# Queries and keys of pairs 4 to 9 loaded by casting DMAs, the third weight issued earlier, and the feed-forward units around the second batch dealt differently

## The chip, the cores and the metric

The kernel runs on one core of one Trainium2 chip. The metric is the device time of one execution in microseconds (us). Engines are named as in the profile: PE (TensorE), DVE (VectorE), ACT (ScalarE), POOL (GpSimd), SP (SyncE). SP and ACT issue hardware DMAs, POOL issues software DMAs, and only POOL's convert the type on the way.

## The reference

Attention with a few extra keys ("beacons") in front, causal over the rest, is followed by a feed-forward layer that takes the largest of three products.

```python
B, H, S, Nb, D = (8, 8, 576, 16, 64)
k_all = np.concatenate([beacon_k, k], axis=2)
v_all = np.concatenate([beacon_v, v], axis=2)
scores = (1.0 / np.sqrt(D)) * np.matmul(q, k_all.transpose(0, 1, 3, 2))
scores = np.where(causal, -1000000000.0, scores)      # beacons always visible
a = np.exp(scores - scores.max(-1, keepdims=True))
a /= a.sum(-1, keepdims=True) + 1e-09
x = np.matmul(a, v_all).transpose(0, 2, 1, 3).reshape(4608, 512)
h = np.maximum(np.maximum(x @ w1, x @ w2), x @ w3)    # 512 -> 768
out = h @ w_out                                       # 768 -> 512
```

All inputs and the output are float32; the kernel computes in bf16 with float32 accumulation.

## The kernel before

The eight heads of a batch are taken as four *pairs* of heads, numbered through all batches: pairs 0 to 3 are batch 0, 4 to 7 batch 1, 8 to 11 batch 2 and so on to 31 (`PPB` is 4, the pairs of a batch). For each pair the kernel needs queries and keys with the head dimension on the partitions. They reach that form in one of two ways. For batches 0 to 3 PE transposes them: `turn_pair` does 12 transposes of 96 tokens each into two PSUM banks, and `evac_k` and `evac_q` copy the banks into the tiles `kT` and `qT`. From batch 4 on (`B_PE`) a DMA transposes them by way of DRAM.

From batch 1 on, a pair goes through these steps.

- `load_pair` (SP) loads q and k of the pair as float32 into a stage tile `st`, in two DMAs of 288 KB.
- `cast_pair`, or `cast_piece` once for q and once for k, converts them to bf16 on POOL (line 260) into the tiles `p160` and `p161`.
- `turn_pair` transposes (line 387), DVE and ACT copy out (lines 433 and 422).
- `emit_burst` does all 12 score matmuls of the pair (line 495) into all eight PSUM banks, in four groups of two banks; ACT takes the exponentials (line 513).
- `emit_masks` zeroes the causal triangles on POOL (line 535).
- For two pairs together ("a quad") `emit_pv_whole` does 72 matmuls with the values and with ones (line 615); ACT and DVE divide.

Values come by `load_v` on SP, in two pieces per batch, and are converted by `cast_v` on POOL (line 305). The weights come by casting DMAs from POOL: `load_w` (line 327, two DMAs per weight) and `load_w_out` (line 330, one DMA of 768 KB).

The feed-forward work is cut into a fixed list of units; `F(n)` emits the next n of them. Tokens go in blocks of 512. The list of block 0 is: units 0 to 2 (first weight, first half of the tokens, `mm1_halves`, line 720, eight matmuls of 256 columns each), 3 to 5 (second weight, first half), 6 to 11 (the same for the second half), 12 to 17 (third weight, `mm1_unit`, line 691, four matmuls of 512 columns and a maximum on DVE at line 709), 18 to 21 (`mm2_unit`, line 739, six matmuls of 512 columns with `w_out`). Every later block has 22 units too, and their order on PE is the order of emission.

The whole order is written by hand: `start`, `first_batch` (batch 0 in finer steps), `second_batch` (batch 1), then a loop over pairs 8 to 31 that fills the space between the bursts with units up to a fixed count per pair. Each engine takes its own instructions strictly in the order of emission, so a POOL instruction that waits holds up every POOL instruction behind it, DMA issues among them. Eight semaphores serve POOL's DMAs in turn: the issue of a DMA waits until the one eight before it has landed.

In the trace of before, the parts around the change come in this order on PE: the last two products of batch 0 with values, units 3 and 4, the transposes of pair 4, unit 5, and then for each of pairs 4 to 7 a burst, the next pair's transposes and two units (after pair 7's burst: four units, then `emit_pv_whole` for pairs 4 and 5, the transposes of pair 8, two units). Pair 8's burst, `emit_pv_whole` for pairs 6 and 7, unit 18 (the first with `w_out`), the transposes of pair 9 and unit 19 follow.

Of the kernel before, what the change touches and what calls it, by code (L numbers as in the profile page):

```python
# [17 lines left out]
def kernel(  # L18
# [85 lines left out]
    def place(p):  # L104
        b, pi = divmod(p, PPB)
        return b, pi // PPQ, 2 * (pi % PPQ)

    const = ctx.enter_context(tc.tile_pool(name="const", bufs=1))
    st_pool = ctx.enter_context(tc.tile_pool(name="st", bufs=8))
    pair_pool = ctx.enter_context(tc.tile_pool(name="pair", bufs=4))  # L110
    half_pool = ctx.enter_context(tc.tile_pool(name="half", bufs=2))
    v_pool = ctx.enter_context(tc.tile_pool(name="v", bufs=2))
# [105 lines left out]
    def load_pair(p, gate=None):  # L218
        b, g, j0 = place(p)
        hs = slice(head(g, j0), head(g, j0) + 2)  # L220
        st = new_stage(("pair", p))
        if gate:
            gate.memset(st[0:QP, 0:1], 0.0)
        for i, src in enumerate((q, k)):
            nc.sync.dma_start(
                out=st[0:QP, i * NQ2 : (i + 1) * NQ2].rearrange("p (h x) -> p h x", h=2),
                in_=src[b, hs].rearrange("h (p r) d -> p h (r d)", r=QR),
            )
# [14 lines left out]
    def cast_half(p, i, cast):  # L243
        t16 = half_pool.tile([QP, HR, 2, D], BF16, name=f"h16{i}")
        cast(t16.rearrange("p r h d -> p h r d"), stage.pop(("half", p, i)))
        stage["half16", p, 0, i] = (t16.rearrange("p r h d -> p r (h d)"),)

    def load_quad(g, h):
        for i in range(2):
            t16 = const.tile([QP, 4, HR, D], BF16, name=f"quad{g}{h}{i}")  # L250
            nc.gpsimd.dma_start(
                out=t16.rearrange("p h r d -> p h (r d)"), in_=half_source(g, h, i, 0, 4)
            )
            for j in range(PPQ):
                stage["half16", PPQ * g + j, h, i] = (t16[:, 2 * j], t16[:, 2 * j + 1])

    def cast_piece(p, i, cast):
        st = stage["pair", p]
        t16 = pair_pool.tile([QP, QR, 2, D], BF16, name=f"p16{i}")
        cast(  # L260
            t16.rearrange("p r h d -> p h r d"),
            st[0:QP, i * NQ2 : (i + 1) * NQ2].rearrange("p (h r d) -> p h r d", h=2, r=QR),
        )
        stage["pair16", p, i] = t16

    def cast_pair(p, q_cast, k_cast):
        cast_piece(p, 0, q_cast)
        cast_piece(p, 1, k_cast)
        stage.pop(("pair", p))
# [98 lines left out]
    def store_pair(p):  # L368
        b, pi = divmod(p, PPB)
        for i, dst in enumerate((q_dram[b][pi], k_dram[b][pi, Nb:NK])):  # L370
            src = stage.pop(("pair16", p, i))
            nc.sync.dma_start(
                out=dst.rearrange("(p r) x -> p (r x)", r=QR),
                in_=src.rearrange("p r h d -> p (r h d)"),
            )

    def fetch_pair(p):
# [4 lines left out]


    def turn(p, i, ps):
        src = stage.pop(("pair16", p, i))
        for r in range(QR):
            nc.tensor.transpose(  # L387
                ps[:, r * QP : (r + 1) * QP],
                src[:, r].rearrange("p h d -> p (h d)"),
                ident[0:QP, 0:QP],  # L390
            )

    def fill(at_bank, n):
        for _ in range(n):
# [274 lines left out]
    def finish_pv():  # L669
        invert_sums()  # L670
        multiply()
# [143 lines left out]
    def cast_step(p):  # L815
        return (p - 2, 0) if p < B_PE * PPB else (p - 5, int(p < 19))
# [6 lines left out]
            load_beacons(B_PE, B, bk32)  # L823
        load_pair(p, **gate)

    loads = [(cast_step(p), 2 * (p >= B_PE * PPB), partial(load_turned_pair, p)) for p in range(2 * PPB, NPAIR)]
    loads += [(v_step(b, i), 1, partial(load_v, b, i)) for b in range(2, B) for i in range(2)]
    loads = [load for _, _, load in sorted(loads, key=lambda x: x[:2])]

    def next_load(n=1, **gate):  # L830
        for _ in range(n):
            if loads:
                loads.pop(0)(**gate)
# [51 lines left out]
    def first_batch():  # L885
        S_(0, 0)
        T(2, 0, 0, 6)
        S_(1, 0)
        T(2, 0, 1, 7, None, 3)
        T(3, 0, 0, 4)  # L890
        T(3, 0, 1, 5)
        V(0)
        V(1)
        load_w(0, [0])
        fill(6, 2)
        S_(2, 0)
# [24 lines left out]
        P(0, 0, 0, 1)  # L921
        S_(1, 2)
        M(0, 3, True)
        P(0, 0, 1)
        M(1, 1)
        invert_sums()
        S_(1, 3)
        P(1, 0, apart=True)
        M(1, 2)
        invert_sums()  # L930
        multiply(3)
        M(1, 3, True)
        load_w(1, [1])
        S_(2, 1)
        by_pool(bk16_1, bk32_1)
        multiply()
        load_pair(PPB, nc.vector)
        for p in range(PPB + 1, 2 * PPB):
            load_pair(p)
        load_v(1, 0)  # L940
        load_v(1, 1)
        next_load()
        S_(2, 2)
        P(0, 1)
        S_(2, 3)
        M(2, 1)
        invert_sums()
        F()
        S_(3, 1)
        M(2, 2)  # L950
        multiply()
        F()
        S_(3, 2)
        M(2, 3, True)
        S_(3, 3)
        M(3, 1)
        M(3, 2)
        M(3, 3, True)
        F()
        turn_beacons(1, B_PE, bk16_1)  # L960
        cast_pair(PPB, by_pool, by_pool)
        P(1, 1)
        finish_pv()
        F(2)
        turn_pair(PPB, by_act)
        place_beacons(PPB, by_act)
        cast_pair(PPB + 1, by_pool, by_pool)
        load_w(2)
        F()
        free_banks[:] = [2, 3, 0, 1, 4, 5, 6, 7]  # L970

    def second_batch():
        for p in range(PPB, 2 * PPB):
            place_beacons(p + 1, by_act)
            emit_burst(p)
            for gi in range(NG):
                emit_masks(p, gi)
                if p < PPB + 2 and 0 < gi < 3:
                    cast_piece(p + 2, gi - 1, by_pool)
                if p == 2 * PPB - 1 and gi == 1:  # L980
                    cast_v(1, 1, by_pool)
                    next_load(gate=nc.gpsimd)
                    next_load(3)
            if p < PPB + 2:
                stage.pop(("pair", p + 2))
            if p == PPB + 2:
                load_w_out()
                cast_v(1, 0, by_pool)
            if p + 1 < 2 * PPB:
                turn_pair(p + 1, by_dve)  # L990
                F(2, next_psum)
        F(4, next_psum)
        for p in range(2 * PPB, 2 * PPB + 2):
            cast_pair(p, by_pool, by_pool)
            next_load()
        finish = emit_pv_whole(n_quad)
        turn_pair(2 * PPB, by_dve)
        F(2, next_psum)
        finish()
# [93 lines left out]
```

## Time and profile before

| | |
|---|---|
| median of 3 runs (lowest, highest) | 286.55 us (285.75, 287.72) |
| the profiled execution: time, span | 285.18 us, 283.5 us |
| PE busy | 274.7 us (97%), 2996 matmuls |
| DVE, ACT, POOL busy | 172.7 us, 159.4 us, 136.4 us |
| L260, the casts of q and k on POOL | 56 instructions, 44.7 us, 821 ns each |
| L387, the transposes of q and k on PE | 144 matmuls, 8.6 us |
| software DMA queue (POOL) | 4048 packets, 4.03 MB, 9.0% of 16 engines' span |
| hardware DMA queue (SP) | 80672 packets, 45.76 MB, 71.8% |

The span is the time between the first and the last profiled instruction of the program; the 1.7 us around it belong to the execution's time. PE's busy time is a model of overlapped matmuls, so a busy PE need not be at its peak; where a wait matters, the start of the next matmul says more. Stretches in the text are in us from the start of the span.

### The profile page before, as it was taken

Reading aid. Unit: us, or ns where it says so; the run is one execution under the profiler, and the core shown is the slowest. Engines: PE = TensorE matmul, PEld = TensorE weight load, DVE = VectorE, ACT = ScalarE, POOL = GpSimd, SP = SyncE. Lnnn points to the kernel's source line nnn. Section 1 sums busy time; section 2 is a strip of 40 time slices with the busy share of each in tenths; the row PEclk is TensorE's granted clock in tenths of the full one; section 3 lists DMA queues with packets and bytes.
Section 4 is the critical chain, followed back from the end, with each engine's and each line's share of the span. In section 5 each row is a group of like instructions: output and inputs, shape, how many; then the busy total and the mean of one; then the engine's idle time right before and its main releaser. Section 6 shows DMA issues by size and latency. Waiting matters only on the chain.

```text
span 283.5 us, 7622 instructions
## 1 busy us (share of the span) xinstructions
PE 274.7 (97%) x2996; PEld 156.4 (55%) x2996; DVE 172.7 (61%) x303; ACT 159.4 (56%) x299; POOL 136.4 (48%) x282
## 2 busy tenths in 40 slices
PE   7889999999999999999999999999999999999995
PEld 3466664555555555555556787555555554444442
DVE  3774765583856658274836383638363847876873
ACT  3697595896668576858585858585767640000000
POOL 7263789287376865466556746583346210000000
PEclk9999999999999999999999999999999999999999
DMA  7999999999999999999999999999451003004004
GB/s 146 193 198 222 246 225 178 240 201 295 276 226 235 255 265 203 226 222 240 250 213 225 267 254 183 216 258 218 121 156 39 0 2 146 2 1 150 0 0 148
DMA packets 85315, 50.59 MB, mean 178 GB/s; under 512 B 64416, under 2 KB 80032, under 8 KB 85280
## 3 DMA queue, kind: packets, MB, share of 16 engines
q1 hardware_dynamic: 80672, 45.76, 71.8%
q0 software_dynamic: 4048, 4.03, 9.0%
q8 instruction: 23, 0.38, 0.6%
q10 hardware_dynamic: 560, 0.33, 0.5%
q14 instruction: 12, 0.10, 0.1%
HBM read 35.13 MB, written 14.22 MB: 174 GB/s over the span
## 4 chain that ended last, share of the span: by engine, by line
PE 82%; DVE 1%; issue 0%
PE acc L691 46%; PE acc L739 16%; PE acc L615 11%; PE acc L495 7%; PE acc L387 2%; PE acc L757 0%; DVE hT L709 0%; DVE qT L422 0%; DVE y L764 0%; DVE kT L433 0%
## 5 line engine op out<-in xcount | busy, mean ns | idle before, releaser
L691 PE MATMUL acc<-xT,w_sb 128*128 128x512 bf16 (+4 forms) x744 | 135.3, 338 | 0.0
L709 DVE TENSOR_TENSOR hT<-hT,acc 128x512 bf16<-128x512 bf16 x102 | 70.0, 687 | 59.2 <-PE acc L691 50.0
L691 PEld LDWEIGHTS <-w_sb 128*128 128x128 bf16 x744 | 69.2, 98 | 59.7
L535 POOL TENSOR_SCALAR_AFFINE_SELECT at_sb<-at_sb 128x256 bf16<-128x256 bf16 (+2 forms) x176 | 62.8, 378 | 71.1 <-ACT at_sb L513 69.4
L513 ACT ACTIVATE at_sb<-acc 128x208 bf16<-128x208 f32 (+3 forms) x140 | 89.5, 737 | 5.9 <-PE acc L495 4.6
L260 POOL CAST p<-st 96x768 bf16<-96x768 f32 x56 | 44.7, 821 | 9.3 <-PE acc L615 5.1
L739 PE MATMUL acc<-w_out_sb,hT 128*128 128x512 bf16 (+2 forms) x246 | 48.4, 348 | 0.0
L711 ACT CAST hT<-acc 128x352 bf16<-128x352 f32 x18 | 8.1, 452 | 47.0 <-PE acc L691 47.0
L739 PEld LDWEIGHTS <-hT 128*128 128x128 bf16 x246 | 22.6, 98 | 21.7 <-DVE hT L709 1.6
L746 DVE COPY y<-acc 128x512 f32<-128x512 f32 (+1 forms) x35 | 21.9, 628 | 20.5 <-PE acc L739 14.8
L711 DVE CAST hT<-acc 128x512 bf16<-128x512 f32 (+1 forms) x48 | 26.6, 554 | 9.4 <-PE acc L691 9.1
L495 PE MATMUL acc<-qT,kT 64*128 64x208 bf16 (+1 forms) x336 | 26.9, 280 | 1.1 <-DVE hT L730 0.6
L764 ACT COPY y<-acc 128x320 f32<-128x320 f32 x1 | 0.4, 426 | 46.0 <-PE acc L757 46.0
L495 PEld LDWEIGHTS <-kT 64*128 64x128 bf16 x336 | 15.5, 94 | 13.3 <-issue 2.6
L615 PE MATMUL acc<-at_sb,v_sb 128*32 128x512 bf16 (+5 forms) x672 | 22.8, 281 | 0.0
L638 DVE TENSOR_TENSOR xT<-raw,recip 128x576 bf16<-128x576 f32 x28 | 21.8, 821 | 0.0
L625 ACT COPY raw<-acc 128x512 f32<-128x512 f32 x28 | 15.8, 637 | 4.5 <-PE acc L615 4.3
L305 POOL CAST v_sb<-st 128x1536 bf16<-128x1536 f32 (+2 forms) x21 | 18.3, 893 | 0.0
L615 PEld LDWEIGHTS <-v_sb 128*32 128x32 bf16 (+1 forms) x672 | 14.5, 96 | 6.7
L489 ACT ACTIVATE at_sb<-acc 128x1024 bf16<-128x1024 f32 (+3 forms) x16 | 13.1, 860 | 3.6 <-PE acc L480 3.5
L615 PE MATMUL acc<-at_sb,ones 128*32 128x512 bf16 (+3 forms) x336 | 14.9, 284 | 0.0
L433 DVE COPY kT<-acc 128x576 bf16<-128x576 bf16 x12 | 9.0, 752 | 6.3 <-PE acc L387 6.3
(69 smaller groups left out, 170.5 us busy)
## 6 DMA issues: line engine op xcount, KB each, us to landing
out_dram<-y SPq DMA_DIRECT2D x35, 256.0 KB, 3.5
st<-in_q_dram SPq DMA_DIRECT2D x28, 288.0 KB, 5.3
st<-in_k_dram SPq DMA_DIRECT2D x28, 288.0 KB, 5.5
st<-in_v_dram SPq DMA_DIRECT2D x24, 256.0 KB, 6.7
w_sb<-in_moe_w_dram POOLq DMA_DIRECT2D x6, 384.0 KB, 7.7
q_dram<-p SPq DMA_DIRECT2D x16, 144.0 KB, 2.3
k_dram<-p SPq DMA_DIRECT2D x16, 144.0 KB, 2.3
st<-in_v_dram SPq DMA_DIRECT2D x8, 224.0 KB, 6.4
```

The source lines that it names most:

```text
L260: cast(t16.rearrange("p r h d -> p h r d"), st[0:QP, i * NQ2 : (i + 1) * NQ2].rearrange("p (h r d) -> p h r d", h=2, r=QR),)
L305: cast(v_sb[0:n, t:t1].rearrange("p t h d -> p (t h d)"), st[0:n, (t - t_lo) * H * D : (t1 - t_lo) * H * D],)
L495: nc.tensor.matmul(ps, kTs[p % NT][hs, 128 * t : 128 * t + 128], qTs[p % NT][hs, q0:q1], start=True, stop=True, tile_position=(64 * e, 0),)
L513: nc.scalar.activation(out=both_heads(p, gi)[:, e0:e1], in_=acc[:, first + e0 : first + e1, 0 : g_width(p, gi)], func=AF.Exp, scale=scale,)
L535: nc.gpsimd.affine_select(out=view, in_=view, compare_op=ALU.is_ge, fill=0.0, base=x0, pattern=[[0, 2], [1, hi - lo]], channel_multiplier=-1,)
L615: nc.tensor.matmul(acc[32 * j : 32 * j + 32, bank, lo + q0 - qa : lo + qb - qa], lhsT, at_view(PPQ * quad + j // 2, t, j % 2, q0, qb), sta ...
L638: nc.vector.tensor_mul(xT[:, 2 * g + i, c0 : c0 + S], raw[:, i], recip)
L691: nc.tensor.matmul(ps[:, a:b], w_in[i][:, ct, 128 * ft : 128 * (ft + 1)], xT[:, ct, x0 : x0 + b - a], start=(ct == 0), stop=(ct == n_ct - 1),)
L709: nc.vector.tensor_max(h[:, lo:hi], h[:, lo:hi], ps[:, lo:hi])
L711: (by_act if hi < TOKB else by_dve)(h[:, lo:hi], ps[:, lo:hi])
L739: nc.tensor.matmul(ps[:, lo:hi], hT[:, ft, 128 * tt : 128 * (tt + 1)], w_out_sb[:, ft, lo:hi], start=(ft == 0), stop=(ft == n_ft - 1),)
L746: (by_act if hi < d_model else by_dve)(y[:, lo:hi], ps[:, lo:hi])
```

## The change

- `load_cast` is new. It loads q and k of a pair by two casting DMAs from POOL, 288 KB of float32 each, straight into bf16 tiles. There is no stage tile and no cast on POOL. The tiles are those that `load_quad` fills for batch 0, now two larger ones per quad that are used again by later pairs.
- Pairs 4 to 9 go this way. The loads of pairs 4 to 7 are issued in `first_batch` between POOL's masks of batch 0; those of pairs 8 and 9 at the end of `second_batch`: pair 8's right after pair 7's burst, pair 9's after `load_w_out`.
- In the new tiles each head lies by itself, so `turn` does 24 transposes of 64 columns of weights for such a pair, two side by side on the array, in place of 12 of 128.
- `load_w(2)`, the third weight, moves from behind the casts of pairs 4 and 5 to behind the load of pair 7.
- `load_w_out` moves from the end of pair 6 (before `cast_v(1, 0)`) to the middle of pair 7's masks, behind `cast_v(1, 1)`.
- `load_v` of batch 1 moves from the middle of `first_batch` to behind pair 4's transposes, gated by a DVE memset. The list of later loads starts at pair 10 rather than 8.
- Units: one unit (not two) ahead of pair 4's transposes and two (not one) behind; three instead of two after the bursts of pairs 4 and 5; two instead of four after that of pair 7. By the product of pairs 4 and 5 with the values, 16 units are out in both kernels.
- The stage pool has seven tiles instead of eight.

```diff
-    st_pool = ctx.enter_context(tc.tile_pool(name="st", bufs=8))
+    st_pool = ctx.enter_context(tc.tile_pool(name="st", bufs=7))
...
+    quads = [
+        [const.tile([QP, 2 * 4, HR, D], BF16, name=f"quad{g}{i}") for i in range(2)] for g in range(n_quad)
+    ]
+
+    def load_cast(p):
+        b, g, j0 = place(p)
+        for i, src in enumerate((q, k)):
+            t16 = quads[g][i][:, 2 * j0 : 2 * j0 + 4]
+            nc.gpsimd.dma_start(
+                out=t16.rearrange("p (h s) r d -> p h (s r d)", h=2),
+                in_=src[b, head(g, j0) : head(g, j0) + 2].rearrange("h (p r) d -> p h (r d)", r=QR),
+            )
+            rows = t16.rearrange("p (h s) r d -> p h (s r) d", h=2)
+            stage["pair16", p, i] = (rows[:, 0], rows[:, 1])
...
     def turn(p, i, ps):
-        src = stage.pop(("pair16", p, i))
+        heads = stage.pop(("pair16", p, i))
+        n = 128 // len(heads)
         for r in range(QR):
-            nc.tensor.transpose(
-                ps[:, r * QP : (r + 1) * QP],
-                src[:, r].rearrange("p h d -> p (h d)"),
-                ident[0:QP, 0:QP],
-            )
+            for e, src in enumerate(heads):
+                nc.tensor.transpose(
+                    ps[n * e : n * e + n, r * QP : (r + 1) * QP],
+                    src[:, r],
+                    ident[0:QP, 0:QP],
+                    tile_position=(0, n * e),
+                )
...
-    loads = [... for p in range(2 * PPB, NPAIR)]
+    loads = [... for p in range(2 * PPB + 2, NPAIR)]
...
         load_w(1, [1])
+        load_cast(PPB)
         S_(2, 1)
         by_pool(bk16_1, bk32_1)
         multiply()
-        load_pair(PPB, nc.vector)
-        for p in range(PPB + 1, 2 * PPB):
-            load_pair(p)
-        load_v(1, 0)
-        load_v(1, 1)
-        next_load()
         S_(2, 2)
         P(0, 1)
         S_(2, 3)
         M(2, 1)
+        load_cast(PPB + 1)
         invert_sums()
         F()
         S_(3, 1)
         M(2, 2)
+        load_cast(PPB + 2)
...
         M(3, 1)
         M(3, 2)
+        load_cast(PPB + 3)
+        load_w(2)
         M(3, 3, True)
         F()
         turn_beacons(1, B_PE, bk16_1)
-        cast_pair(PPB, by_pool, by_pool)
         P(1, 1)
         finish_pv()
+        F()
+        turn_pair(PPB, by_act)
+        load_v(1, 0, nc.vector)
+        load_v(1, 1)
+        place_beacons(PPB, by_act)
         F(2)
-        turn_pair(PPB, by_act)
-        place_beacons(PPB, by_act)
-        cast_pair(PPB + 1, by_pool, by_pool)
-        load_w(2)
-        F()
...
         for p in range(PPB, 2 * PPB):
+            last = p == 2 * PPB - 1
             place_beacons(p + 1, by_act)
             emit_burst(p)
+            if last:
+                load_cast(2 * PPB)
             for gi in range(NG):
                 emit_masks(p, gi)
-                if p < PPB + 2 and 0 < gi < 3:
-                    cast_piece(p + 2, gi - 1, by_pool)
-                if p == 2 * PPB - 1 and gi == 1:
+                if last and gi == 1:
                     cast_v(1, 1, by_pool)
+                    load_w_out()
+                    load_cast(2 * PPB + 1)
                     next_load(gate=nc.gpsimd)
-                    next_load(3)
-            if p < PPB + 2:
-                stage.pop(("pair", p + 2))
-            if p == PPB + 2:
-                load_w_out()
+                    next_load(4)
+            if p == 2 * PPB - 2:
                 cast_v(1, 0, by_pool)
-            if p + 1 < 2 * PPB:
+            if not last:
                 turn_pair(p + 1, by_dve)
-                F(2, next_psum)
-        F(4, next_psum)
-        for p in range(2 * PPB, 2 * PPB + 2):
-            cast_pair(p, by_pool, by_pool)
-            next_load()
+            F(3 if p < PPB + 2 else 2, next_psum)
         finish = emit_pv_whole(n_quad)
         turn_pair(2 * PPB, by_dve)
         F(2, next_psum)
```

More of the change, by code (lines that the diff above doesn't have):

```diff
@@ L246, in cast_half @@
         stage["half16", p, 0, i] = (t16.rearrange("p r h d -> p r (h d)"),)
+    quads = [
[11 more added lines that the diff above has]
+            stage["pair16", p, i] = (rows[:, 0], rows[:, 1])
     def load_quad(g, h):
         for i in range(2):
-            t16 = const.tile([QP, 4, HR, D], BF16, name=f"quad{g}{h}{i}")
+            t16 = quads[g][i][:, 4 * h : 4 * h + 4]
             nc.gpsimd.dma_start(
@@ L263, in cast_piece @@
         )
-        stage["pair16", p, i] = t16
+        stage["pair16", p, i] = (t16.rearrange("p r h d -> p r (h d)"),)
     def cast_pair(p, q_cast, k_cast):
@@ L370, in store_pair @@
         for i, dst in enumerate((q_dram[b][pi], k_dram[b][pi, Nb:NK])):
-            src = stage.pop(("pair16", p, i))
+            (src,) = stage.pop(("pair16", p, i))
             nc.sync.dma_start(
                 out=dst.rearrange("(p r) x -> p (r x)", r=QR),
-                in_=src.rearrange("p r h d -> p (r h d)"),
+                in_=src.rearrange("p r x -> p (r x)"),
             )
@@ L384, in turn @@
     def turn(p, i, ps):
-        src = stage.pop(("pair16", p, i))
+        heads = stage.pop(("pair16", p, i))
+        n = 128 // len(heads)
         for r in range(QR):
-            nc.tensor.transpose(
-                ps[:, r * QP : (r + 1) * QP],
-                src[:, r].rearrange("p h d -> p (h d)"),
-                ident[0:QP, 0:QP],
-            )
+            for e, src in enumerate(heads):
[5 more added lines that the diff above has]
+                )
     def fill(at_bank, n):
@@ L824, in load_turned_pair @@
         load_pair(p, **gate)
-    loads = [(cast_step(p), 2 * (p >= B_PE * PPB), partial(load_turned_pair, p)) for p in range(2 * PPB, NPAIR)]
+    loads = [(cast_step(p), 2 * (p >= B_PE * PPB), partial(load_turned_pair, p)) for p in range(2 * PPB + 2, NPAIR)]
     loads += [(v_step(b, i), 1, partial(load_v, b, i)) for b in range(2, B) for i in range(2)]
```

## The prediction

> **What bounds the kernel now.** I read the page's totals and its chain first, then PE's timeline, then POOL's beside it, then the DMA rows.
>
> ```profile
> PE 274.7 (97%) x2996; PEld 156.4 (55%) x2996; DVE 172.7 (61%) x303; ACT 159.4 (56%) x299; POOL 136.4 (48%) x282
> ...
> PE 82%; DVE 1%; issue 0%
> ```
>
> PE is busy for 97%, and the chain runs through PE from 43.7 us to the end with only a few waits between. So PE's stream is the time: a gap that is closed before the end is a gain, and every new gap is a loss that nothing later makes good. POOL, busy for 48%, is no bound in itself.
>
> ```profile
> 29.18 0.42 PE L387 MATMUL acc<-ident,p 96*128 96x96 bf16 x6
> 30.06 0.43 PE L387 MATMUL acc<-ident,p 96*128 96x96 bf16 x6 [0.47 <-POOL p L260]
> 30.33 1.04 PE L720 MATMUL acc<-xT,w_sb 128*128 128x256 bf16 x8
> ...
> 32.44 0.98 PE L387 MATMUL acc<-ident,p 96*128 96x96 bf16 x12
> 33.26 1.91 PE L720 MATMUL acc<-xT,w_sb 128*128 128x256 bf16 x16
> 35.10 0.81 PE L495 MATMUL acc<-qT,kT 64*128 64x208 bf16 x7
> 36.20 0.36 PE L495 MATMUL acc<-qT,kT 64*128 64x336 bf16 x5 [0.28 <-DVE hT L728]
> 36.50 0.69 PE L387 MATMUL acc<-ident,p 96*128 96x96 bf16 x12
> ...
> 47.57 0.87 PE L615 MATMUL acc<-at_sb,ones 128*32 128x512 bf16 x20
> ...
> 49.82 0.83 PE L387 MATMUL acc<-ident,p 96*128 96x96 bf16 x12
> ```
>
> Starts are compared. Twelve transposes take 0.52 us when nothing holds them (36.50 to 37.02). Pair 4's take 1.15 us (29.18 to 30.33) and pair 5's 0.82 (32.44 to 33.26), for POOL's casts come late. A burst takes 0.85 us later in the chain, but 1.40 in batch 1 (35.10 to 36.50), since its last bank waits for DVE's copies of the two units ahead. That is what can be won: 0.63 + 0.30, and 0.55 for each of three bursts.
>
> ```profile
> 42.48 0.93 POOL L535 TENSOR_SCALAR_AFFINE_SELECT at_sb<-at_sb 128x256 bf16<-128x256 bf16 x3 [0.60 <-ACT at_sb L513]
> 43.36 0.85 POOL L330 DMA_DIRECT2D w_out_sb<-in_moe_w_out_dram  x1
> 44.21 1.48 POOL L305 CAST v_sb<-st 128x1536 bf16<-128x1536 f32 x1
> 45.63 0.76 POOL L535 TENSOR_SCALAR_AFFINE_SELECT at_sb<-at_sb 128x256 bf16<-128x256 bf16 x2
> 46.34 1.16 POOL L305 CAST v_sb<-st 128x512 bf16<-128x512 f32 x2
> ```
>
> This is POOL around pair 7's burst (42.62 on PE). Pair 6's last masks follow ACT's last exponential at once, so POOL cannot come sooner to what stands behind them. The weight `w_out` is issued at 43.36.
>
> ```profile
> w_sb<-in_moe_w_dram POOLq DMA_DIRECT2D x6, 384.0 KB, 7.7
> ...
> w_out_sb<-in_moe_w_out_dram POOLq DMA_DIRECT2D x1, 768.0 KB, 11.4
> quad<-in_q_dram POOLq DMA_DIRECT2D x3, 144.0 KB, 7.3
> quad<-in_k_dram POOLq DMA_DIRECT2D x3, 144.0 KB, 8.1
> ```
>
> The last column is the time from issue to landing. `w_out` landed at 54.8, 1.1 us before PE's first matmul with it at 55.91. A casting DMA on POOL's queue is no quick thing.
>
> **The change part by part.** *POOL's casts of pairs 4 to 9* go: 12 of 0.82 us, 9.8 us in all. Twelve DMA issues come at 0.55 to 0.67 us (w_sb and quad rows), some 7 us. Off the path both; what counts is when data is there.
>
> *Pair 4.* Its loads are issued behind the last half of the second weight (POOL 20.1) and no stage loads compete until 30. By the slowest cast row (9.7 us) they land at 30.5, by the quad medians at 28.5; PE comes at about 28.8, so no wait is taken. That saves 0.63. Against it, four issues of pairs 5 and 6 stand before POOL's last masks of batch 0, which ended at 25.5 and move to 26.5; PE's product with values needs them at 26.2: 0.4 lost. The transposes are 24 in place of 12. The old half-width rows took 0.38 us for 12 and 0.51 for 18, so about 0.71 for 24: 0.2 more. (Bounds: 0, if two side by side cost one, and 0.25.) Pair 4's burst stays at 31.3.
>
> *To the product of pairs 4 and 5.* Pairs 5 to 7 are issued at 23.4 to 27.6 and needed at 32, 37 and 41: in time even at 9.7 us. The third weight is issued at 27.6 instead of 32.9, the last unit of the second weight needs no wait in either. With three units DVE has 2.76 us for copies instead of 1.84, and the wait in the bursts of pairs 5 and 6 falls from 0.55 to some 0.15; pair 7's, with two units ahead, keeps it. Sum: 0.30 (pair 5) and 0.8 (two bursts) won, three sets of transposes at 0.2 lost, four units moved but none added: 0.7 with the odd tenths of the unit rows (0.92 and 0.87). So the product starts at 46.9 instead of 47.64. Bounds: -2.5 if every wait goes, 0 if DVE's lag stays.
>
> *Pair 8's load* is the first loss. Pair 6's burst now starts at 40.3; ACT's exponentials end 3.55 us later (0.36 + 3.19, as in before), masks 1.0, `cast_v` 1.48: POOL comes to the two issues at 46.3 and 46.9. PE wants the data at 46.9 + 2.25 (L615) = 49.2, less than 3 us later. No cast landed in under 5.7 us, with much else in flight; the system is quiet here, and the same 288 KB on SP's queue landed in 3.4 and 3.6 us when it was (issues at 87.9 and 88.4). I take 4.1, nearer the quiet rows: k lands at 51.0 and the transposes end at 51.35, against 49.7 without a wait: 1.65 lost. Bounds: 0.95 at 3.4 us, 3.3 at 5.7.
>
> *w_out* is the second. It goes behind pair 8's two issues, two masks (0.76) and `cast_v(1, 1)` (1.16): issue at 49.4 instead of 43.4. PE comes to unit 18 at 51.35 + 5.5 (50.41 to 55.91 in before) = 56.85. The nearest rows are `w_out` itself, 11.4, and the two halves of the third weight, together the same 768 KB, 9.9 (issue at 32.88, second landing at 42.74). Middle 10.6: landing at 60.0, 3.15 lost. Bounds: nothing at 5.7 (the fastest w_sb, half the size), 4 at 11.4. The cover before was the 12.5 us from issue to use; now it is 7.4.
>
> *Pair 9's load* stands behind `w_out` in POOL's queue (50.3 to 51.4). In 5.7 us that queue moved `w_out`:
>
> ```profile
> q0 software_dynamic: 759, 0.77, 92.5%
> ```
>
> (stretch 45.8 to 51.5: packets, MB, share). So 0.29 MB more is 2.2 us: it lands near 62, and PE comes to its transposes at 61.3. With 0.2 for the transposes 0.5 is lost (0.2 to 2). SP's later loads start 2.7 us later (51 instead of 48.4) under a PE that is 4 to 5 later: nothing. The masks of pair 7 end at 52 on POOL and are needed at 54: hidden. Seven stage tiles suffice, as two pairs fewer are staged.
>
> Sum: -0.7 + 1.65 + 3.15 + 0.5 = +4.6 us. On the profiled execution that is 285.18 + 4.6 = 289.8; that execution lies 1.37 us under the median of the runs, so the median after is 286.55 + 4.6 = 291.1.
>
> Two rules of the Trainium skill beside this. "DMA: Bandwidth & Descriptors" (section on the anatomy of one DMA, SWDGE path) puts a DMA from GpSimd at about 2.0 us plus its bytes over 436 GB/s; the 1.57 MB read for `w_out` would then be 5.6 us, where the trace shows 11.4. By the rule unit 18 would not wait at all and the sum would be near +1. "TensorE: Matmul & The Clock Gate" (Part 1, the HAM clock gate) says that after an idle window of about 3.4 us the array runs at half rate until it has been busy as long; no run here shows it yet, for the granted clock is 1.00 in every stretch and no wait of PE passes 1.5 us. By that rule a wait of 3.2 us might cost up to 1.7 us more, an estimate from its figures, and the sum would be +6.3.
>
> **The rivals.** *Loads land quickly* (not slower). Pair 8's in 3.4 us, `w_out` in under 7.4, since nothing is in flight when it is issued, and only SP's loads from 51 on stretch it. For it: the bulk of `w_out`, 0.77 of 0.79 MB, went in 5.7 us, and the first 2.4 us after its issue showed one packet, with a pair's load still moving. Against it: the last packets trailed for 3.3 us under SP's loads, which now come 1.6 us after the issue rather than 4.2. Then -0.7 + 0.95 + 0.2 = +0.45: 287.0. It decides below 7.4 us from issue to landing of `w_out`.
>
> *All of PE's old gaps go and no new one comes* (faster). All of what can be won, 0.93 + 1.65, and side by side transposes free, loads in time: -2.6, or 284.0. For it: DVE's and ACT's busy shares leave room. Against it: pair 8's load comes to POOL under 3 us before its use.
>
> *POOL is held longer* (much slower). The values of batch 1 are issued at 31 instead of 28.1 and their first piece landed 15.6 us after the first issue. Again 15.6 us puts it at 46.6, POOL's cast of it waits 1.8 us, and with it pair 8, `w_out` at 11.4 and pair 9: +7.2, or 293.8. Against it: what kept those loads so long, four pairs on the same queue, is gone.
>
> **How the numbers follow.** Forecast 0.48 (own range 288.8 to 293), quick landing 0.28, longer hold 0.14, no gaps 0.10. One per cent, 2.9 us, is about what a measurement of this kernel can tell from no change; the bounds are 283.7 and 289.4. Slower: 0.14 and 0.44 of the forecast's 0.48: 0.58. Same: 0.28 and the other 0.04: 0.32. Faster: 0.10. The range runs from 286.2, under the quick landing, to 294.8, over the longer hold, and leaves out most of the no-gap case and the ends of the others. Predicted: 291.1.
>
> **What would show it.** Right: PE's line 739 starts first near 60, with a wait for the DMA of `w_out`; the transposes of pair 8 wait 1 to 2 us for a quad DMA; the product of pairs 4 and 5 starts near 46.9; bursts of pairs 5 and 6 take about 1.0 us; 24 transposes take 0.7. Wrong: `w_out` lands within 7 us of its issue, or POOL issues pair 8's load much before 46, or the bursts keep their 1.4 us, or PE's clock leaves 1.00.

## The result and the profile after

| | before | after |
|---|---|---|
| median of 6 runs (lowest, highest) | 285.98 us (285.19, 287.72) | 289.65 us (288.42, 291.65) |
| ratio of after to before, 95% interval | | 1.0127 (1.0094 to 1.0159) |
| the profiled execution: time, span | 285.18 us, 283.5 us | 290.40 us, 288.7 us |

The changed kernel is slower, by 3.7 us at the median. The prediction had named 291.1 us in a range of 286.2 to 294.8. The lines of the file have moved: the transposes of line 387 are now line 404, the score matmuls (495) line 513, the products with values (615) line 633, the units with `w_out` (739) line 757, the masks (535) line 553, the casts of values (305) line 320. The tiles of the cast queries and keys are now called `quad`.

First the totals of the page after, and the chain that ended last.

```profile
PE 277.3 (96%) x3068; PEld 157.3 (54%) x3068; DVE 172.3 (60%) x303; ACT 159.6 (55%) x299; POOL 136.7 (47%) x282
...
PE 85%; DMA 6%; POOL 2%; DVE 2%; issue 2%; ACT 1%; POOLq 0%; DVEq 0%; ACTq 0%
```

The span grew by 5.2 us and PE's busy time by 2.6, with 72 more matmuls (half-width transposes). Part of the time is therefore idle PE, and part is work that took longer. Before, the chain from 43.7 us on was PE, but for 2.7 us (50.7 to 53.4) that went through DVE's copies; now 6% of it is DMA. The chain in order of time says where: one piece is a load in the start phase, and the other this.

```profile
48.22 1.10 POOL v_sb L320 x2
50.74 9.92 DMA quad<-in_k_dram
61.15 2.65 PE acc L757 x12
```

The chain comes through a cast of values on POOL, then through the issue of pair 9's keys at 50.74 and their 9.92 us to landing. PE's timeline shows the waits themselves (start, length, line, count, and in brackets the idle time with what ended it).

```profile
28.62 0.70 PE L404 MATMUL acc<-ident,quad 96*64 96x96 bf16 x24
...
36.57 0.39 PE L513 MATMUL acc<-qT,kT 64*128 64x336 bf16 x6 [0.24 <-DVE hT L746]
...
47.07 0.86 PE L633 MATMUL acc<-at_sb,ones 128*32 128x512 bf16 x20
...
48.83 0.27 PE L633 MATMUL acc<-at_sb,v_sb 128*32 128x208 bf16 x4 [0.34 <-POOL v_sb L320]
49.38 0.90 PE L633 MATMUL acc<-at_sb,v_sb 80*32 80x80 bf16 x24 [0.28 <-POOL v_sb L320]
...
50.30 0.70 PE L404 MATMUL acc<-ident,quad 96*64 96x96 bf16 x24
...
57.22 1.47 PE L757 MATMUL acc<-w_out_sb,hT 128*128 128x512 bf16 x6 [0.82 <-DMA w_out_sb<-in_moe_w_out_dram]
59.07 0.45 PE L404 MATMUL acc<-ident,quad 96*64 96x96 bf16 x12 [0.38 <-DMA quad<-in_q_dram]
60.71 0.45 PE L404 MATMUL acc<-ident,quad 96*64 96x96 bf16 x12 [1.19 <-DMA quad<-in_k_dram]
61.08 2.72 PE L757 MATMUL acc<-w_out_sb,hT 128*128 128x352 bf16 x12
63.74 1.27 PE L513 MATMUL acc<-qT,kT 64*128 64x208 bf16 x12
```

Up to 47.07 PE has gained 0.50 us on before (47.57). Part of this comparison is the start phase, which differs from execution to execution: the first product of batch 0 with values begins at 16.40 before and 17.00 after, ahead of the first load that moved (19.68). Counted from unit 3 (27.36 and 27.65), the way to the product takes 20.21 us before and 19.42 after, so the gain of this stretch is 0.8 us. Then PE waits for POOL in the middle of the product with values, for `w_out`, and twice for pair 9. And POOL's timeline shows why each of these comes late:

```profile
44.73 1.46 POOL L320 CAST v_sb<-st 128x1536 bf16<-128x1536 f32 x1
46.14 0.67 POOL L256 DMA_DIRECT2D quad<-in_q_dram  x1
46.80 0.65 POOL L256 DMA_DIRECT2D quad<-in_k_dram  x1
47.45 0.78 POOL L553 TENSOR_SCALAR_AFFINE_SELECT at_sb<-at_sb 128x256 bf16<-128x256 bf16 x2
48.16 1.16 POOL L320 CAST v_sb<-st 128x512 bf16<-128x512 f32 x2
49.27 0.85 POOL L345 DMA_DIRECT2D w_out_sb<-in_moe_w_out_dram  x1
50.11 0.65 POOL L256 DMA_DIRECT2D quad<-in_q_dram  x1
50.74 0.64 POOL L256 DMA_DIRECT2D quad<-in_k_dram  x1
```

The second cast of values (48.16) stands behind pair 8's two issues and two masks. `w_out` stands behind that cast, and pair 9 behind `w_out`. By the records of the single DMAs, pair 8's load landed 3.26 and 3.29 us after its issues, `w_out` 7.91 us after its own, and pair 9's 8.92 and 9.92.

Counted by PE's starts, the 5.2 us add up so:

| part | before | after | shift so far | the part alone |
|---|---|---|---|---|
| product of pairs 4 and 5 | 47.57 | 47.07 | -0.50 | -0.50 |
| transposes of pair 8 | 49.82 | 50.30 | +0.48 | +0.98 |
| unit 18, the first with `w_out` | 55.91 | 57.22 | +1.31 | +0.83 |
| unit 19, behind pair 9's transposes | 57.73 | 61.08 | +3.35 | +2.04 |
| unit 20, behind pair 9's burst | 59.98 | 64.94 | +4.96 | +1.61 |

(0.2 us more come after it.) The last part is no wait. Twelve score matmuls took 1.27 us at 63.74, and 0.92 before (59.14). The windows of after give the reason (behind the five engines stand the granted clock, the DMA's share and GB/s; the first window is used further below).

```profile
44.00:46.00 2.00, 1.80 (x16) 0.92 (x17) 0.88 (x2) 1.72 (x4) 2.00 (x4) 1.00 0.00 0
...
60.00:62.00 2.00, 1.29 (x16) 0.81 (x17) 0.74 (x1) 0.30 (x2) 0.82 (x1) 0.79 1.17 238
62.00:64.00 2.00, 2.00 (x14) 1.30 (x14) 0.11 (x2) 0.45 (x1) 0.00 (x0) 0.50 1.33 213
64.00:66.00 2.00, 2.00 (x17) 0.88 (x14) 1.57 (x3) 1.81 (x4) 1.17 (x2) 0.86 1.12 208
```

PE's clock was halved from 61.15 to 64.56, for 3.41 us, which costs half of that, 1.7 us, where PE has work throughout. After it PE runs as before, some 5 us late to the end. Not every execution has this stretch: the spans of the six runs are 286.7, 287.1, 287.2, 288.7, 288.9 and 289.9 us, and the two with a mean clock of 1.00 are 286.7 and 287.1. One such stretch in an execution makes a mean clock of 0.994.

### The profile page after: what moved, and what is told of

Same layout as the page of the kernel before. It is cut to its first block, busy times and chain, and to the rows that moved or that the text cites. A ratio compares the mean times of both kernels' runs of the same rounds, so it can differ in the third digit from the quotient of the medians.

```text
span 288.7 us, 7758 instructions
## 1 busy us (share of the span) xinstructions
PE 277.3 (96%) x3068; PEld 157.3 (54%) x3068; DVE 172.3 (60%) x303; ACT 159.6 (55%) x299; POOL 136.7 (47%) x282
## 4 chain that ended last, share of the span: by engine, by line
PE 85%; DMA 6%; POOL 2%; DVE 2%; issue 2%; ACT 1%; POOLq 0%; DVEq 0%; ACTq 0%
PE acc L709 44%; PE acc L757 16%; PE acc L633 9%; PE acc L513 7%; DMA quad<-in_k_dram 6%; PE acc L738 4%; PE acc L404 2%; PE acc L600 1%; DVE at_sb L551 1%; PE acc L498 1%; POOL quad L256 1%; POOL at_sb L553 1%; POOL v_sb L320 1%; ACT at_sb L531 0%; DVE kT L433 0%
## 5 line engine op out<-in xcount | busy, mean ns | idle before, releaser
L553 POOL TENSOR_SCALAR_AFFINE_SELECT at_sb<-at_sb 128x256 bf16<-128x256 bf16 (+2 forms) x176 | 64.4, 386 | 85.8 <-ACT at_sb L531 79.6
L757 PE MATMUL acc<-w_out_sb,hT 128*128 128x512 bf16 (+2 forms) x246 | 49.7, 355 | 0.8 <-DMA w_out_sb<-in_moe_w_out_dram 0.8
L275 POOL CAST p<-st 96x768 bf16<-96x768 f32 x44 | 35.0, 822 | 1.9 <-DMA st<-in_q_dram 1.0
L757 PEld LDWEIGHTS <-hT 128*128 128x128 bf16 x246 | 23.2, 100 | 23.2 <-DVE hT L727 1.6
L656 DVE TENSOR_TENSOR xT<-raw,recip 128x576 bf16<-128x576 f32 x28 | 20.9, 788 | 0.0
```

Source lines behind the costliest of these rows:

```text
L275: cast(t16.rearrange("p r h d -> p h r d"), st[0:QP, i * NQ2 : (i + 1) * NQ2].rearrange("p (h r d) -> p h r d", h=2, r=QR),)
L553: nc.gpsimd.affine_select(out=view, in_=view, compare_op=ALU.is_ge, fill=0.0, base=x0, pattern=[[0, 2], [1, hi - lo]], channel_multiplier=-1,)
L656: nc.vector.tensor_mul(xT[:, 2 * g + i, c0 : c0 + S], raw[:, i], recip)
L757: nc.tensor.matmul(ps[:, lo:hi], hT[:, ft, 128 * tt : 128 * (tt + 1)], w_out_sb[:, ft, lo:hi], start=(ft == 0), stop=(ft == n_ft - 1),)
```

## The experiments

**The theories.** The first ("theory 1" below): the loss is the lateness of what POOL does around pair 7's burst. Casting loads placed there hold up the values' cast and `w_out`, and `w_out` holds up pair 9; moved forward, where nothing waits, the loss goes. A rival: the casting loads themselves or the doubled number of transposes cost time, wherever they stand. A second rival: the waits are small and PE's halved clock behind them is the loss. A third ("theory 2"): the new deal of units is to blame.

**Issue `w_out` earlier**, among pair 6's masks.

```diff
                 emit_masks(p, gi)
+                if p == 2 * PPB - 2 and gi == 1:
+                    load_w_out()
                 if last and gi == 1:
                     cast_v(1, 1, by_pool)
-                    load_w_out()
                     load_cast(2 * PPB + 1)
```

> The changed kernel with one edit: w_out is issued among pair 6's masks (POOL near 42.5 us) instead of behind the second cast of the values of batch 1 (49.3). Theory 1 (the loss is made of separate waits of PE for things that POOL issues or casts too late: values 1.0, w_out 0.9, pair 9's load 2.0, and a half-rate stretch of the PE clock that the last two cause): the wait for w_out goes, pair 9's load no longer stands behind it and lands some 3 to 5 us after its issue near 49.5, so its wait goes too, and the clock stays at 1.00. Pair 8's load now stands behind w_out in the queue and may cost 0 to 1.5 us in its place. The wait for the values stays. Time over the kernel before: +0.5 to +2 us (ratio 1.002 to 1.007). Rival (the loss is in the casting loads and the 24 transposes themselves, wherever they are issued): the ratio stays near 1.013.

Measured: 287.04 us against 285.46, ratio 1.0048 (1.0014 to 1.0082); the profiled span is 284.5. PE's timeline of this kernel:

```profile
48.22 0.27 PE L633 MATMUL acc<-at_sb,v_sb 128*32 128x208 bf16 x4 [0.33 <-POOL v_sb L320]
...
49.99 0.45 PE L404 MATMUL acc<-ident,quad 96*64 96x96 bf16 x12 [0.22 <-DMA quad<-in_q_dram]
50.77 0.45 PE L404 MATMUL acc<-ident,quad 96*64 96x96 bf16 x12 [0.33 <-DMA quad<-in_k_dram]
...
56.54 1.47 PE L757 MATMUL acc<-w_out_sb,hT 128*128 128x512 bf16 x5
57.94 0.70 PE L404 MATMUL acc<-ident,quad 96*64 96x96 bf16 x24
```

The waits for `w_out` (landed 7.41 us after its issue at 41.84) and for pair 9 (3.5 us) are gone, and with them over half of the loss. The wait for the values' cast stays, and pair 8, now behind `w_out`, takes 4.4 and 4.5 us and waits 0.55 in all. Moving the one 768 KB load helped two transfers at once.

**Issue pairs 8 and 9 earlier**, one each after the masks of pairs 4 and 5; `w_out` stays behind the values' cast.

```diff
-            if last:
-                load_cast(2 * PPB)
             for gi in range(NG):
...
                     load_w_out()
-                    load_cast(2 * PPB + 1)
...
+            if p < PPB + 2:
+                load_cast(p + PPB)
             if p == 2 * PPB - 2:
                 cast_v(1, 0, by_pool)
```

> The changed kernel with pair 8's load issued after pair 4's masks and pair 9's after pair 5's (POOL near 35.7 and 40.2 us, where it idles), w_out left where it is behind the cast of the values. Theory 1: without two issues (1.3 us) ahead, the cast of the values' second piece ends near 48 and PE's wait for it goes; w_out is issued 1.3 us sooner, near 48, and lands near 56, so at most 0.3 us of its wait is left; pair 9's wait is gone and the clock stays at 1.00. Time: before minus 0.5 (the earlier product) plus 0.3 (transposes of pairs 8 and 9): within 0.5 us of before, ratio 0.997 to 1.003. Rival (casting loads and transposes cost it wherever they are issued): 1.008 or more.

Measured: 287.06 us, ratio 1.0048 (1.0015 to 1.0081), above the expected interval. The waits for values, pair 8 and pair 9 are gone, and one is longer:

```profile
48.99 0.70 PE L404 MATMUL acc<-ident,quad 96*64 96x96 bf16 x24
...
57.00 1.47 PE L757 MATMUL acc<-w_out_sb,hT 128*128 128x512 bf16 x5 [1.92 <-DMA w_out_sb<-in_moe_w_out_dram]
58.40 0.70 PE L404 MATMUL acc<-ident,quad 96*64 96x96 bf16 x24
```

`w_out` is issued at 47.64, 1.6 us sooner than in the changed kernel, and lands at 56.95, only 0.2 us sooner: 9.31 us on the way. SP's next loads begin 1.0 us after its issue here (48.63), and 2.2 us after it in the changed kernel (51.52). Nothing else that stands in its way is new, so these loads are the likely cause; no run moved them alone, and the last section compares all twelve traces. PE, which now has no wait ahead, runs into it.

**Both together**: `w_out` among pair 6's masks, pairs 8 and 9 after those of pairs 4 and 5 (the two diffs above).

> Both edits: pairs 8 and 9 issued after the masks of pairs 4 and 5, w_out among pair 6's masks. Theory 1: no wait of PE for a DMA or for POOL is left between 28 and 70 us, the clock stays at 1.00, and the time is that of before minus the gain ahead of the product of pairs 4 and 5 (0.5 us) plus 0.3 for the transposes of pairs 8 and 9: 0 to 0.5 us under before, ratio 0.997 to 1.000, and no different from the kernel with only the pairs moved by more than 0.3 us. Rival: 1.008 or more.

Measured: 285.67 us against 285.46, ratio 0.9998 (0.9969 to 1.0027).

```profile
49.47 0.70 PE L404 MATMUL acc<-ident,quad 96*64 96x96 bf16 x24
...
55.50 1.47 PE L757 MATMUL acc<-w_out_sb,hT 128*128 128x512 bf16 x5
56.90 0.70 PE L404 MATMUL acc<-ident,quad 96*64 96x96 bf16 x24
57.53 1.48 PE L757 MATMUL acc<-w_out_sb,hT 128*128 128x352 bf16 x12
```

No PE wait for a DMA or for POOL is left between 28 and 70 us, and the whole loss is gone. The kernel still has all casting loads, all half-width transposes and the new deal of units, so the rival that these cost time by themselves falls, as far as the interval tells (0.3%, some 0.8 us). It also shows how little there was to win: unit 20 starts at 59.80, 0.18 us before that of the kernel before, or 0.6 us when both are counted from their unit 3 (27.80 here, 27.36 before).

**Fill PE's wait** before pair 9's turn with nine matmuls whose output nobody reads (they write to the bank that pair 9's transposes write next), so that PE does not stand idle there.

```diff
                 n += 1
+                if n == 1 and p == 2 * PPB:
+                    fill(free_banks[0], 9)
                 if n == 1 and p + 1 < B_PE * PPB:
```

> The changed kernel with nine more matmuls of 512 columns on constant data (1.9 us), written to the bank that pair 9's transposes write next, put on PE between unit 18 and those transposes, where PE waits for pair 9's load. No result depends on them. If the half-rate stretch of the clock (61.1 to 64.6 in the profile after) comes from PE's idleness in the waits, the granted clock stays at 1.00 in every run and the time falls by about 1.7 us against those runs of the changed kernel that had the stretch and by nothing against those that had none; the waits for w_out and pair 9's load stay as they are: ratio to before about 1.009. If the clock falls for another reason, it still falls to half after 60 us and the ratio stays at 1.013 or rises.

Measured: 289.23 us, ratio 1.0110 (1.0064 to 1.0157). It overlaps with that of the changed kernel, so the same kernel was run again, beside the changed one unaltered (289.11 us, ratio 1.0128, 1.0093 to 1.0163):

> The changed kernel with nine matmuls on constant data (512 columns, no result depends on them) between unit 18 and pair 9's transposes, once more. Theory: no half-rate stretch after 57 us, so the spans stay under 288.4 in all runs, and the median is 0.3 to 1 us under that of the changed kernel run beside it; without the theory, runs of 288.7 and more are as frequent as there.

> The changed kernel once more, for the spread of its runs by granted clock. Theory (PE's waits between 56 and 61 us may or may not fill a window after which the clock is halved for 3.4 us): some runs with a mean clock of 1.000 and a span near 287, others with 0.994 or less and a span near 288.8, 1.7 us more. If the half-rate stretch cost nothing, spans would not differ by clock.

Measured for the filled kernel: 289.56 us, ratio 1.0142 (1.0110 to 1.0174). It is no faster; the expected gain did not come. The nine matmuls did stand where PE would have waited (first run; their line 413 is `fill`):

```profile
58.92 2.10 PE L413 MATMUL acc<-busy 128*128 128x512 bf16 x9
60.95 0.84 PE L404 MATMUL acc<-ident,quad 96*64 96x96 bf16 x24
```

In both profiled executions with the fill the clock was full from 50 us on (and halved for one or two stretches in batch 0, between 14 and 22 us, where the run with the old deal, below, had one as well). In the changed kernel's repeat it was full throughout, and the waits alone made the loss:

```profile
49.33 0.28 PE L633 MATMUL acc<-at_sb,v_sb 128*32 128x208 bf16 x4 [0.35 <-POOL v_sb L320]
49.88 0.90 PE L633 MATMUL acc<-at_sb,v_sb 80*32 80x80 bf16 x24 [0.28 <-POOL v_sb L320]
...
57.90 1.47 PE L757 MATMUL acc<-w_out_sb,hT 128*128 128x512 bf16 x5 [1.01 <-DMA w_out_sb<-in_moe_w_out_dram]
59.65 0.45 PE L404 MATMUL acc<-ident,quad 96*64 96x96 bf16 x12 [0.28 <-DMA quad<-in_q_dram]
61.41 0.45 PE L404 MATMUL acc<-ident,quad 96*64 96x96 bf16 x12 [1.31 <-DMA quad<-in_k_dram]
```

Over both groups of runs, the changed kernel's twelve spans are 286.7 to 287.8 us eight times and 288.7 to 289.9 four times. The halved clock explains the profiled execution's last 1.6 us, and it can explain the upper spans, but it is not what the median is made of. The record of all executions says the same: a mean clock of 0.994 or less stands beside 21 of the 59 executions of the kernel before that were timed with these experiments, and beside 5 of the changed kernel's 12. Among the others (0.997 and more) the median span is 283.6 us before and 287.1 after, so at full clock 3.5 us of loss remain. The halved clock falls as the cause of the loss.

**Cast the values first**: both pieces of values right behind each other, then pair 8's load.

```diff
-            if last:
-                load_cast(2 * PPB)
...
                 if last and gi == 1:
-                    cast_v(1, 1, by_pool)
                     load_w_out()
...
             if p == 2 * PPB - 2:
                 cast_v(1, 0, by_pool)
+                cast_v(1, 1, by_pool)
+                load_cast(2 * PPB)
```

> The changed kernel with the second cast of the values of batch 1 right behind the first and pair 8's load behind both (issues near 47.3 and 48.0 us instead of 46.1 and 46.8). Theory 1 (POOL owes PE four things within a few us, and each waits behind the others): PE's product of pairs 4 and 5 no longer waits for the values (1.0 us won), and pair 8's transposes wait in their place, for the load lands 3.3 us after its issue, q near 50.6 and k near 51.3, where PE comes at 49.4: 1.3 to 2 us lost. The waits for w_out and pair 9 stay, 0.3 to 0.8 us shorter. Time within 1 us of the changed kernel. Rival (the values are late because SP loads them late): the product still waits, for a DMA of the values.

Measured, one profiled run: 291.26 us. The wait moved as expected and did not shrink:

```profile
50.35 0.45 PE L404 MATMUL acc<-ident,quad 96*64 96x96 bf16 x12 [1.11 <-DMA quad<-in_q_dram]
51.36 0.45 PE L404 MATMUL acc<-ident,quad 96*64 96x96 bf16 x12 [0.56 <-DMA quad<-in_k_dram]
...
59.66 1.47 PE L757 MATMUL acc<-w_out_sb,hT 128*128 128x512 bf16 x6 [0.97 <-DMA w_out_sb<-in_moe_w_out_dram]
```

The values' wait is gone, but pair 8's issues come 1.0 us later (47.12 and 47.78), and that load, at 3.2 and 3.5 us, is waited for instead. The waits for `w_out` (0.97) and pair 9 (0.34 and 1.26) did not get shorter, although that had been expected. Here too the clock was halved for 3.41 us, from 51.81 on; the changed kernel's profiled execution, which had such a stretch as well, took 290.40 us, 0.9 us less. The order of POOL's steps at this place decides only which of them is late.

**Pair 9 ahead of `w_out`.**

```diff
                     cast_v(1, 1, by_pool)
-                    load_w_out()
                     load_cast(2 * PPB + 1)
+                    load_w_out()
```

> The changed kernel with pair 9's load issued before w_out. Theory 1 (POOL's queue is served in order, and what stands behind w_out waits for its 768 KB): pair 9's load lands 3.3 to 4.5 us after its issues at 49.3 and 49.9, near 53, and PE does not wait for it; w_out is issued at 50.6 and lands 8 to 9.5 us later, near 59, and unit 18 waits 2 to 3.5 us instead of 0.8. The sum of the two waits falls from 2.9 to about 2.8: time within 1 us of the changed kernel. Rival (pair 9's load is slow by itself or by SP's loads that start at 51.5): it still lands 8 us or more after its issue.

Measured, one profiled run: 291.41 us.

```profile
60.11 2.44 PE L757 MATMUL acc<-w_out_sb,hT 128*128 128x512 bf16 x6 [3.58 <-DMA w_out_sb<-in_moe_w_out_dram]
62.48 1.17 PE L404 MATMUL acc<-ident,quad 96*64 96x96 bf16 x24
```

Pair 9 now lands 3.5 us after its issues, in place of 9 to 10, and is not waited for. `w_out`, issued 1.4 us later than in the changed kernel (50.68), takes 9.39 us. So the long landing of pair 9 was its place behind `w_out` in POOL's queue. The wait of 3.58 us was followed by a halved clock, from 60.46 to 63.87: the same 6 matmuls with `w_out` take 2.44 us instead of 1.47. Against the changed kernel's profiled execution (290.40 us, also with a halved stretch) the time is 1.0 us longer.

**The old deal of units**: two units after each of pairs 4 to 6 and four after pair 7, as before.

```diff
-            F(3 if p < PPB + 2 else 2, next_psum)
+            F(4 if last else 2, next_psum)
```

> The changed kernel with the units dealt as before the change around the second batch: two after the bursts of pairs 4 and 5 and four after that of pair 7. Theory 2 (the new deal itself makes POOL late: with two units moved ahead of pair 7's burst, pair 6's exponentials and with them all that POOL does behind its masks come 1.7 us later, while PE has 1.7 us less to do before it needs them): POOL comes to pair 8's load near 44.5, the wait for the values goes, w_out is issued near 47.6 and pair 9's load near 48.5, so the waits for w_out and pair 9 fall from 2.9 to between 0 and 1.5 us. PE's bursts of pairs 5 and 6 take 1.4 us again (0.2 more each). Ratio to before 1.002 to 1.006. Theory 1 alone (only the order on POOL's queue counts): waits of the same size, ratio 1.012 to 1.014.

Measured: 288.47 us against 285.54, ratio 1.0095 (1.0062 to 1.0129), above the expectation of theory 2 and below that of theory 1 alone. The values' cast and pair 8 are not waited for. Counted from unit 3, POOL begins that cast 18.8 us later in place of 20.5, while PE comes to the product after 19.5 us (19.4 in the changed kernel). The rest stays:

```profile
56.80 1.47 PE L757 MATMUL acc<-w_out_sb,hT 128*128 128x512 bf16 x6 [0.49 <-ACT raw L643]
58.57 0.45 PE L404 MATMUL acc<-ident,quad 96*64 96x96 bf16 x12 [0.30 <-DMA quad<-in_q_dram]
60.35 0.45 PE L404 MATMUL acc<-ident,quad 96*64 96x96 bf16 x12 [1.34 <-DMA quad<-in_k_dram]
```

The profile puts unit 18's wait down to ACT, but `w_out` landed at 56.75, 0.05 us ahead of the unit's start, as close as in the other traces where it is waited for. Bursts 5 and 6 take 1.26 and 1.28 us here, not the 1.4 expected, and the way from unit 3 to the product is only 0.07 us longer: the new deal won next to nothing ahead of the product. So it is behind the values' wait, about 1 us of the loss by the medians (whose intervals overlap), and no more; where POOL's DMAs stand makes the larger part.

**ACT copies the queries of pairs 5 and 6**, on top of the kernel with both moved forward, to give DVE time for the copies of the units ahead.

```diff
-                turn_pair(p + 1, by_dve)
+                turn_pair(p + 1, by_act if p < PPB + 2 else by_dve)
```

> The kernel with all three loads early (pairs 8 and 9 after the masks of pairs 4 and 5, w_out among pair 6's masks), and ACT instead of DVE copies out the queries of pairs 5 and 6, which takes 0.65 us off DVE ahead of each of the bursts of pairs 5 and 6. If DVE's lag is what stretches those bursts from 0.85 to 1.22 us, they take 0.9 to 1.0 and the kernel is 0.3 to 0.6 us faster than without it, 0.998 of before. If the bursts wait for ACT's exponentials instead, they grow and it is slower by as much.

Measured: 285.89 us, ratio 1.0000 (0.9971 to 1.0028). Nothing moved: bursts 5 and 6 still take 1.23 and 1.22 us, with waits of 0.24 and 0.23 for DVE's `hT`. DVE's copies of queries are not what makes it late. PE's timeline and DVE's show what does:

```profile
37.44 0.38 PE L513 MATMUL acc<-qT,kT 64*128 64x336 bf16 x6 [0.24 <-DVE hT L746]
...
36.70 0.69 DVE L746 CAST hT<-acc 128x512 bf16<-128x512 f32 x1 [0.25 <-PE acc L738]
```

DVE stands idle until PE has finished the last unit, and PE goes on with the burst 0.05 us after DVE has copied that unit's result (36.70 + 0.69). This copy begins 0.17 us after the burst here (36.53), as much in the changed kernel (35.65 and 35.82), and 0.37 before the change (35.10 and 35.47). So a lag of DVE was worth 0.2 us, which the changed kernel had won already; the rest of the wait is the last unit's own copy.

## Why the prediction was right, and which terms were not

The direction and the kind of loss were right: waits for what POOL brings too late, seen at the named places. The total was near for an execution without the halved clock, +3.35 against +4.6, but the terms behind it differ more than the total does, so that the total came so near is in part luck: two terms were too high, one was too low and one was missing. Of the signs that the prediction named for being wrong, one came: the clock left 1.00 in the profiled execution. Of those for being right, pair 8's wait and the bursts of 1.0 us did not come.

- *The gain ahead of the product* (-0.7): -0.8 seen, counted from unit 3, and its parts were off both ways and cancelled. Up to pair 4's burst, forecast unchanged, 0.53 us were won (3.99 us from unit 3 before, 3.46 after), and only 0.26 behind it. The 0.4 us for POOL's late masks of batch 0 was not lost: that product took 1.79 us (1.81 before). The transposes of pair 4 took 0.64 us (28.62 to 29.26) for 24; with 0.52 for 12 before, the halves cost 0.12 and not 0.2. The rows that the prediction used (0.38 for 12, 0.51 for 18) give 0.64 when the step between them is carried on. Bursts 5 and 6 took 1.23 and 1.22 us and not 1.0: DVE's lag, which was to give 0.4 in each, gave 0.2, by the last run.
- *Pair 8's load* (+1.65): no wait. The issues came as forecast (46.14 and 46.80 against 46.3 and 46.9). The landing took 3.3 us in place of 4.1, close to the lower bound, and PE itself was 0.98 us late from the values. Without that delay PE would have been at these transposes at 49.32, with the keys landing at 50.09: an estimate from these rows is some 0.5 us of loss, a third of the term. With the values first, pair 8 was waited for after all, 1.67 us, its issues being 1.0 us later: the need was there, and the other wait covered it.
- *The values' cast* was the step that the sum lacked (+0.98). The sum moved `w_out` behind `cast_v(1, 1)` and priced that; it did not ask who waits for `cast_v(1, 1)` itself, now behind two issues of 1.32 us together, nor that the new deal, with two units moved ahead of pair 7's burst, brings POOL to it 1.7 us later (20.5 us behind unit 3, against 18.8 with the old deal). PE's product needs that piece 1.4 us after its start (48.49).
- *`w_out`* (+3.15): 0.83. The issue came as forecast (49.27 against 49.4); the landing was 7.9 us in place of 10.6. The first rows taken, 11.4 and 9.9, had SP's loads and the pairs' beside them. Between 44 and 46 us the DMA share of after is 0.00 (the first of the windows above), and at its issue only the last 0.8 us of pair 8's load was under way, until SP's loads came at 51.5. The quick-landing rival had this mechanism right, and put its point of decision at 7.4 us; 7.4 was reached only where `w_out` was issued among pair 6's masks. The longer hold did not come: the first piece of the values landed at 39.47, long before POOL's cast of it at 44.73.
- *Pair 9* (+0.5): 2.04. Its landing near 62 was forecast, and 60.66 seen. But with `w_out` sooner, PE came to it sooner too (58.7, not 61.3). The two terms share one mechanism: what is not waited for at `w_out` is waited for right behind it.
- *The clock* was given a place, but no part in the sum. The halved stretch came, about as long and as dear as the rule had it, yet in the profiled execution it followed waits of at most 1.19 us each. "TensorE: Matmul & The Clock Gate" of the Trainium skill (Part 1, the HAM clock gate) puts it on an idle window of about 3.4 us. The run with 3.58 us of wait agrees. The changed kernel does not, and the measurement decides: it shows the stretch without such a window, PE being busy 54% of the 3.41 us ahead of it, while its repeat shows none although PE is busy only 52% of a window as long (58.04 to 61.45).
- The rule of "DMA: Bandwidth & Descriptors" (the Trainium skill, section on the anatomy of one DMA, SWDGE path) gives 5.6 us for `w_out`. The 7.9 of the changed kernel lies about midway between that and the 10.6 taken from the rows; no run came under 7.4. For a pair's DMA in a quiet system the rule gives 2.7 (288 KB read), where 3.3 was measured. In both places the measurement is what holds here.

Not settled: when exactly the clock is halved and why the runs of one kernel differ in it; and how much of `w_out`'s landing time is due to SP's loads and how much to what still moves ahead of it.

## What to carry to other kernels

A DMA issued from an engine that also computes is a step in that engine's order: when one is moved, ask what it pushes back, the plain computations among it, and who waits for each of those. In this crowded stretch both reorderings (the values first, pair 9 first) only moved the wait; issuing the loads one to three bursts sooner, where POOL had room, removed all of them. Where two late transfers stand in one queue, price them together: what the first does not cost, the second will.

## What was not expected of the hardware

- One and the same `w_out` transfer landed 7.4 to 11.4 us after its issue. The distance to SP's next loads does not order these times: 7.9 to 8.3 and 10.5 both came with 2.2 to 2.3 us, and 11.4 with 4.2 (before the change). What orders all twelve traces is how long `w_out` was alone, from the landing of the last load ahead of it to the issue of SP's next one (what stands behind it in POOL's own queue not counted): 3.0 us and more with 7.4 to 8.0, 1.4 to 1.5 us with 7.9 to 8.3, 1.0 us with 9.3, and at most 0.1 us with 9.4, 10.5 and 11.4. This was read from the traces afterwards; no run varied it alone.
- A pair's casting load (288 KB read per DMA) landed in 3.2 to 3.5 us where little else moved, and in 8.9 to 12.5 us right behind `w_out`.
- The halved clock came behind one wait of 3.6 us, but also with waits of 0.4 to 1.2 us in a row, and in batch 0 of some runs too. PE's busy share in the 3.41 us ahead does not decide it: 0.54 (the changed kernel) and 0.51 (the values first) came with it, while windows as long with 0.52 (the repeat) and 0.42 (pairs 8 and 9 early) passed at full clock.
